# Layer 2 of one group by seven block products, with the steps around it moved

## The chip, the cores and the metric

The kernel runs on one core of a Trainium2 chip. The core has five engines with a queue each, all issuing in order: PE (TensorE, matmul), DVE (VectorE), ACT (ScalarE), POOL (GpSimd) and SP (SyncE, which here only issues DMAs). The metric is device time in microseconds (us) from start to end of one execution; the time of the kernel is the median of its runs. A profile is of one more execution.

## The reference, cut to what matters

```python
B, H, S, D = 8, 8, 576, 64                       # q, k, v: (B, H, S, D), float32
scores = q @ k.T / sqrt(D)                       # kept where 0 <= row - col < 64
attn   = softmax(scores)                         # the rest is masked out
x      = (attn @ v) with heads side by side      # (B, S, 512)
xn     = (x - mean(x)) / sqrt(var(x) + 1e-6) * g_ln
out    = x + relu(xn @ w_ch1) @ w_ch2            # w_ch1: 512 x 2048, w_ch2: 2048 x 512
```

## The kernel before

**Tiling.** Rows are handled in blocks of 128. The first 512 rows of batch b make group b (four blocks, called kb 0 to 3), and the last 64 rows of all eight batches make group 8. Weights are kept in SBUF as f16, with g_ln multiplied into `w1g`; `w2s` holds W2.

**Attention of one block** goes through these steps, each a function that records instructions:
- `cast_qk` (L139), `cast_v` (L172) and `shift_v` (L187) turn loaded f32 tiles into f16 on POOL. `vA` holds V, and `vB` holds V shifted by 64 rows; from batch 2 on `part_vB` (L190) fills `vB` from `vA` with DMAs on SP.
- `t_main` (L252) transposes Q or K on PE and moves the result from PSUM to SBUF, on ACT for Q and on DVE for K where nothing else is said. From batch 3 on Q goes by DMA transpose on SP.
- `s_pe`, `s_exp`, `s_mask` (L307 to L360): scores on PE, exponential on ACT, mask on DVE.
- `b_pe` (L368): probabilities times V on PE. `b_rows` (L390): division by the row sum, then mean and variance, on DVE.
- `z_step` (L416), `z_act` (L441) and `zt_step` (L446): the rows are normalised into z, and z is transposed into `zT`, four pieces of 128 x 128. Groups 0 and 1 only subtract the mean (on DVE, or on ACT for two blocks) and multiply by 1/std after layer 2, since relu lets a positive row factor pass; `root` (L463) computes that factor on POOL. From group 2 on three small POOL steps give 1/std and -mean/std, and z is fully normalised, on ACT in group 2 and on POOL from group 3 on. From group 2 on (`XZ`) `zT` is written by a DMA transpose, apart from block 3 of groups 3 and 5.

**The two layers of one group** come from `mlp_units` (L470) as a list of units for PE:
- Layer 1: `l1` (L477) computes 128 hidden columns for all 512 rows in 4 matmuls of 128 x 512. `l1_half` (L616) computes 256 hidden columns for 256 rows in 8 matmuls of 128 x 256, so that it can start when two blocks of z are there. Both end with a relu on ACT into `hrT`. The argument `split` says for how many of the 16 column groups the halves are used.
- Layer 2, plain: `l2` (L487), 16 matmuls of 128 x 512 for one block of rows, then `add_out` (L498) on DVE and a store. `l2_three` (L629) does three blocks of group 0 side by side.
- Layer 2, by blocks: `stage` (L577) and `product` (L534) do the 512 x 2048 by 2048 x 512 product as a 2 x 2 product of blocks with seven block products in place of eight. `s_sums` (L519) makes the sums of blocks of `hrT` (sS1 to sS4), `w2_sums` (L808) those of W2 (wT2, wT3, wT4, and one in place in `w2s`). Each product is 16 matmuls of 128 x 256, in two units. The order is 4, 1, 2, 6, 5, 7, 3. Products add up in three PSUM banks A, B and C, and `post` and `post_both` (L561 to L573) add a bank to the rows in `x_norm` on DVE before the bank is used again. Stores of row blocks 2 and 3 follow product 7, those of 0 and 1 product 3.

In the kernel before, group 0 uses `l2_three` and `l2`, group 1 `l2`, and groups 2 to 7 the block products. Group 8 has a plan of its own.

**Order.** There is no scheduler: the order on every queue is the order of the calls. The main loop (L934 to L1153) has one period g for each group. Period g runs the units of group g, and after unit i it runs what `at(i, ...)` put into slot i: mostly the attention of batch g + 1 and loads, casts and transposes for batch g + 2. An instruction at the head of a queue that waits holds back all behind it. `queue_up` (L901) puts a long series of loads and POOL casts into slot 0 of period 0.

**PSUM.** There are eight banks. Layer 1 and 2 take turns with two (`mm`), scores have two (`sc`), one pair belongs to `xps`, and two single banks, t0 and t1, serve transposes, one piece of layer 2 of group 0, and bank C. `t_tile` (L72) deals out t0 and t1 in turn, or only t0 where `tbank["shared"]` is set.

Of the kernel before, what the change touches and what calls it, by code (L numbers as in the profile page):

```python
# [18 lines left out]
def kernel(  # L19
# [21 lines left out]
    XZ = 2  # L41
# [87 lines left out]
    def t_two(b, x, half):  # L129
        src = qk16.pop((b, x, half))  # L130
        c0 = 64 * x + 256 * half
        for a in range(2):
            tp = t_tile([128, 4, 128], f"tp_{b}_{x}_{half}_{a}")
            for i in range(4):
                nc.tensor.transpose(out=tp[:, i, :], in_=src[:, 4 * a + i], identity=ident16)
            evac(a, qkT[b][x][:, 2 * a:2 * a + 2, c0:c0 + 256].rearrange("c h (p j) -> c h p j", j=2),
                 tp[:, :].rearrange("c (h j) p -> c h p j", j=2))

# [251 lines left out]
    def b_rows(g, kb):  # L390
# [22 lines left out]
        if g < 2 and (g, kb) not in ((0, 2), (1, 0)):  # L413
            z_step(g, kb)

    def z_step(g, kb):  # L416
# [4 lines left out]
        if g < 2:  # L421
            if (g, kb) not in ((0, 2), (1, 0)):
                nc.vector.tensor_scalar(out=z, in0=xv, scalar1=mu, scalar2=None, op0=ALU.subtract)
            else:
                nmu = p_blk.tile([128, 3], FP32, tag="rsz", name=f"nmu_{g}_{kb}")[:, 0:1]
                nc.vector.tensor_scalar(out=nmu, in0=mu, scalar1=-1.0, scalar2=None, op0=ALU.mult)
                nc.scalar.activation(out=z, in_=xv, func=AF.Identity, bias=nmu, scale=1.0)
            return
# [5 lines left out]
        if g == 2:  # L434
            rsnm[kb] = (rs, nm)
            return
# [4 lines left out]
    def z_act(g, kb):  # L441
        rs, nm = rsnm[kb]
        nc.scalar.activation(out=zsd[(g, kb)], in_=x_norm[(g, kb // 2)][:, kb % 2, :], func=AF.Identity,
                             bias=nm, scale=rs)

    def zt_step(g, kb, eng="act"):  # L446
# [4 lines left out]
        if XZ <= g and not (kb == 3 and g in (3, 5)):  # L451
            nc.sync.dma_start_transpose(out=zT[g][:, :, 128 * kb:128 * kb + 128], in_=z)
            return
# [16 lines left out]
    def mlp_units(g, split=0, three=False, seven=True):  # L470
# [27 lines left out]
        def add_out(kb):  # L498
            xv = x_norm[(g, kb // 2)][:, kb % 2, :]
            if g < 2:  # L500
                nc.vector.scalar_tensor_tensor(
                    out=xv, in0=ch[kb], scalar=rstd[g][:, kb:kb + 1], in1=xv, op0=ALU.mult, op1=ALU.add,
                )
            else:
                nc.vector.tensor_tensor(out=xv, in0=ch[kb], in1=xv, op=ALU.add)
# [395 lines left out]
    def queue_up():  # L901
# [16 lines left out]
        cast_qk(1, 1)  # L918
        cast_v(1, 2, 3)
        shift_v(64, 2)  # L920
        shift_v(0, 2)
        cast_v(1, 3, 4)
        shift_v(64, 3)
        load_qk(2, 0)
        load_qk(2, 1)
        load_v(2, 0, 4)
# [7 lines left out]
    for g in range(NGRP):  # L934
# [4 lines left out]
        units, s_sums = mlp_units(g, (8, 16)[g] if g < 2 else 0, g == 0, g > 1)  # L939
# [14 lines left out]
        if g == 0:  # L954
# [12 lines left out]
            for c in range(2):  # L967
                at(20, vB_cur, 1, c, 0)
                at(20, vB_prev, 1, c, 0)
            at(22, b_pe, 1, 0)  # L970
            at(22, b_rows, 1, 0)
            at(22, z_step, 1, 0)
            at(23, b_pe, 1, 1, "sc")
            at(23, b_rows, 1, 1)
            at(25, zt_step, 1, 0)
            at(25, t_main, 1, 0, 1, 0)
            at(26, lambda: tbank.update(n=0))
            at(26, t_main, 1, 1, 1, 0)
            at(27, zt_step, 1, 1, "dve")
# [3 lines left out]
            at(27, s_exp, 1, 3, 0, 1)  # L983
            at(28, s_mask, 1, 2)
            at(29, s_mask, 1, 3)
        if g == 1:
# [6 lines left out]
            for c in (0, 2):  # L993
                at(0, cast_v, 2, c, c + 2)
                at(5, part_vB, 2, c)
            at(0, t_main, 2, 0, 0)
            at(1, b_pe, 1, 2, "t")
            at(1, b_pe, 1, 3, "sc")
            at(1, b_rows, 1, 2)
            at(1, b_rows, 1, 3)  # L1000
            at(2, root, 1)
            at(2, t_main, 2, 1, 0)
            at(3, t_main, 2, 0, 1)
            at(4, zt_step, 1, 2)
            at(5, t_main, 2, 1, 1)
            at(6, zt_step, 1, 3)
            at(7, w2_sums, 3, 0, 4)
            at(8, w2_sums, 3, 4, 8)
            at(25, w2_sums, 2, 0, 4)
            at(28, w2_sums, 2, 4, 8)  # L1010
            at(9, s_pe, 2, 0)
            at(9, s_pe, 2, 1, False, "xps")
            at(9, s_exp, 2, 0, 0, 1)
            at(10, s_mask, 2, 0)
            at(11, s_exp, 2, 1, 0)
            at(12, s_exp, 2, 1, 1)
            at(13, s_mask, 2, 1)
            for j in range(4):
                i = (14, 17, 20, 22)[j]
                if j < 3:  # L1020
                    at(i, b_pe, 2, j)
                if j < 2:
                    at(i, s_mm, 2, j + 2)
                    at(i + 1, s_mask, 2, j + 2)
                if j == 2:
                    at(i, b_pe, 2, 3, "sc")
                at(i, b_rows, 2, j)
                at(i, z_step, 2, j)
                at((18, 21, 24, 26)[j], z_act, 2, j)
                at((18, 21, 24, 26)[j], zt_step, 2, j)  # L1030
# [11 lines left out]
            first_scores(3, 30)  # L1042
            for i, (x, half) in zip((12, 24, 18, 28), ((0, 0), (1, 0), (0, 1), (1, 1))):
                at(i, t_main, 3, x, half, 0)
# [3 lines left out]
        if g == 2:  # L1048
            for m, i in enumerate((1, 4)):
                at(4 + 2 * m, w2_sums, i, 0, 4)  # L1050
                at(5 + 2 * m, w2_sums, i, 4, 8)
        if g > 1 and b < B:
# [40 lines left out]
            at(12, b_rows, b, 2)  # L1093
            at(12, z_step, b, 2)
            at(19, b_rows, b, 3)
            at(19, z_step, b, 3)
# [24 lines left out]
        if g > 1:  # L1121
# [24 lines left out]
        for i, u in enumerate(units):  # L1146
            if i == (20 if g > 1 else 17 if g == 0 else -1):
# [34 lines left out]
```

## Time and profile before

| | |
|---|---|
| median of 3 runs (lowest, highest) | 302.48 us (302.23, 303.44) |
| profiled execution: time / span from first to last instruction | 302.3 us / 300.3 us |
| busy over the span: PE / DVE / POOL / ACT | 292.2 / 208.4 / 158.4 / 153.9 us |
| mean granted TensorE clock | 0.995 |
| layer 1 of group 1 starts | 53.57 us |
| layer 1 of group 2 starts | 89.45 us |
| DMA: mean rate over the span | 194 GB/s |

The span of period 1, which the change is about, is thus some 36 us. "Busy" is the sum of an engine's instructions; matmuls are pipelined and their ends are modelled, so PE's rates are better taken from rows of many matmuls in the chain of waits, by dividing a row's length by its count. In the timelines a row is start, length, engine, line, operation, output and inputs, count, and in brackets the idle time ahead of it with what ended that.

### The profile page before, as it was taken

The page shows a single profiled execution, that of the slowest core. Times are in us where ns is not written, and L with a number is a line of the kernel's source. Part 1 is how long each engine was busy: PE and PEld are TensorE (multiplying, and loading weights), DVE is VectorE, ACT ScalarE, POOL GpSimd, SP SyncE. Part 2 cuts the span into 40 slices and gives each one's busy share as a digit, 9 for nine tenths or more (in the row PEclk, how much of TensorE's full clock was granted, in tenths as well). Part 3 has the DMA queues.
Part 4 walks back from the last instruction along what each step waited for, and adds up shares of the span by engine and source line. Part 5 has one row for each costly group of instructions (what it writes and reads, how often), then busy time and mean ns, then how long its engine had stood idle before and what let it go on. Part 6 is the DMA issues. An engine that isn't in the chain of part 4 may idle for free.

```text
span 300.3 us, 7568 instructions
## 1 busy us (share of the span) xinstructions
PE 292.2 (97%) x3067; PEld 195.6 (65%) x3067; DVE 208.4 (69%) x409; ACT 153.9 (51%) x259; POOL 158.4 (53%) x234
## 2 busy tenths in 40 slices
PE   8989999999999999999999999999999999999992
PEld 3557545887544588557854786469646854788881
DVE  1781338865937985488858865698667775879972
ACT  2666646676458525873276438841674056216400
POOL 4787877634633876278518860797048307115200
PEclk9999999999999999999999999999999999999997
DMA  7999999989979998999289999992639396013014
GB/s 191 260 382 335 384 286 289 269 266 306 134 194 297 206 187 128 290 248 177 53 265 289 195 160 270 297 163 48 212 72 157 70 232 146 10 38 121 0 38 105
DMA packets 114020, 58.34 MB, mean 194 GB/s; under 512 B 83649, under 2 KB 104705, under 8 KB 113986
## 3 DMA queue, kind: packets, MB, share of 16 engines
q1 hardware_dynamic: 113696, 57.47, 80.0%
q8 instruction: 24, 0.39, 0.6%
q10 hardware_dynamic: 290, 0.40, 0.5%
q14 instruction: 10, 0.08, 0.1%
HBM read 38.80 MB, written 9.44 MB: 161 GB/s over the span
## 4 chain that ended last, share of the span: by engine, by line
PE 95%; ACT 1%; DVE 1%; issue 0%
PE hps L479 31%; PE pA L556 12%; PE pB L556 8%; PE pC L556 8%; PE hph L621 7%; PE ch L491 6%; PE xps L387 4%; PE sc L340 4%; PE ch L638 4%; PE tp L267 3%; PE lA L677 2%; PE warm L848 2%; PE lC L677 1%; PE ztp L456 1%; PE lB L677 1%; ACT pt L350 1%
## 5 line engine op out<-in xcount | busy, mean ns | idle before, releaser
L479 PE MATMUL hps<-zT,w1g 128*128 128x512 f16 x416 | 94.7, 379 | 0.0
L483 ACT ACTIVATE hrT<-hps 128x512 f16<-128x512 f32 x104 | 62.3, 599 | 41.2 <-PE hps L479 37.8
L479 PEld LDWEIGHTS <-w1g 128*128 128x128 f16 x416 | 39.2, 98 | 45.5 <-issue 2.2
L350 ACT ACTIVATE pt<-sc 128x512 f16<-128x512 f32 x72 | 39.3, 600 | 21.4 <-PE sc L340 20.7
L556 PEld LDWEIGHTS <-sS 128*128 128x128 f16 x448 | 43.3, 98 | 5.0
L431 POOL TENSOR_SCALAR rsz<-mvg 128x1 f32<-128x1 f32 x28 | 9.7, 347 | 67.7 <-DVE mvg L412 65.7
L360 DVE TENSOR_TENSOR pt<-pt,mask 128x1024 f16<-128x1024 f16 x32 | 24.7, 776 | 22.3 <-ACT pt L350 22.3
L145 POOL CAST qk<-qk 128x1024 f16<-128x1024 f32 x30 | 33.0, 1114 | 10.3 <-PE hph L621 4.5
L556 PEld LDWEIGHTS <-hrT 128*128 128x128 f16 x336 | 32.1, 98 | 6.4 <-ACT hrT L483 1.0
L248 ACT COPY qkT<-tp 128x1024 f16<-128x1024 f16 (+1 forms) x18 | 17.4, 964 | 24.7 <-PE tp L267 22.4
L556 PE MATMUL pC<-w2s,sS 128*128 128x256 f16 x224 | 26.9, 273 | 0.0
L556 PE MATMUL pA<-wT,sS 128*128 128x256 f16 x224 | 26.9, 273 | 0.0
L407 DVE TENSOR_TENSOR xn<-xps,rcp 128x256 f32<-128x256 f32 (+1 forms) x50 | 25.8, 539 | 1.2 <-DMA out_dram<-xn 0.5
L409 DVE BATCH_NORM_STATS2 stats<-xn 128x6 f32<-128x512 f32 x36 | 25.0, 695 | 1.2
L530 DVE TENSOR_TENSOR sS<-hrT 128x512 f16<-128x512 f16 (+1 forms) x40 | 24.1, 604 | 1.9 <-ACT hrT L483 1.8
L621 PE MATMUL hph<-zT,w1g 128*128 128x256 f16 x192 | 23.4, 273 | 0.1
L437 POOL TENSOR_SCALAR z<-xn,rsz 128x512 f16<-128x512 f32 x24 | 20.7, 862 | 2.5
L403 DVE RECIPROCAL rcp<-xps 128x4 f32<-128x4 f32 (+1 forms) x50 | 7.9, 181 | 18.4 <-PE xps L387 18.4
L432 POOL TENSOR_TENSOR rsz<-rsz,mhalf 128x1 f32<-128x1 f32 x28 | 18.7, 670 | 2.3
L621 PEld LDWEIGHTS <-w1g 128*128 128x128 f16 x192 | 18.1, 98 | 2.9 <-issue 0.2
L491 PE MATMUL ch<-w2s,hrT 128*128 128x512 f16 x80 | 18.8, 380 | 0.0
L387 PEld LDWEIGHTS <-pt 128*64 128x64 f16 x576 | 11.6, 110 | 10.3 <-issue 6.0
(119 smaller groups left out, 427.9 us busy)
## 6 DMA issues: line engine op xcount, KB each, us to landing
out_dram<-xn SPq DMA_DIRECT2D x33, 256.0 KB, 3.2
qk<-in_q_dram SPq DMA_DIRECT2D x16, 512.0 KB, 6.2
qk<-in_k_dram SPq DMA_DIRECT2D x16, 512.0 KB, 7.2
v<-in_v_dram SPq DMA_DIRECT2D x28, 256.0 KB, 6.3
w2s<-in_moe_w_ch_dram SPq DMA_DIRECT2D x9, 512.0 KB, 8.6
w1s<-in_moe_w_ch_dram SPq DMA_DIRECT2D x4, 512.0 KB, 7.2
tk<-in_k_dram SPq DMA_DIRECT2D x8, 256.0 KB, 4.4
tv<-in_v_dram SPq DMA_DIRECT2D x8, 256.0 KB, 4.8
```

Source lines behind the costliest of these rows:

```text
L145: nc.gpsimd.tensor_copy(out=dst[:, :].rearrange("p (a j) e d -> p a e j d", j=j), in_=t[:, :].rearrange("p (a e j d) -> p a e j d", e=2, j ...
L350: nc.scalar.activation(out=o, in_=i, func=AF.Exp, bias=0.0, scale=scale)
L360: nc.vector.tensor_tensor(out=ptv, in0=ptv, in1=mb, op=ALU.mult)
L387: nc.tensor.matmul(out=tiles[h // n][64 * r:64 * r + 64, h % n, :D + 1], lhsT=pt[:, par, hp, r, :], rhs=rhs, start=True, stop=True)
L407: nc.vector.tensor_tensor(out=xn[:, n * i:n * i + n], in0=xps[:, :, 0:D], in1=rcp_b, op=ALU.mult)
L409: nc.vector.bn_stats(out=stats, in_=xv)
L479: nc.tensor.matmul(out=hps, lhsT=w1g[:, kc, 128 * hc:128 * (hc + 1)], rhs=zT[g][:, kc, :], start=(kc == 0), stop=(kc == NKC - 1),)
L483: nc.scalar.activation(out=hrT[:, hc, :], in_=hps, func=AF.Relu, bias=0.0, scale=1.0)
L491: nc.tensor.matmul(out=ch[kb], lhsT=hrT[:, hc, 128 * kb:128 * (kb + 1)], rhs=w2s[:, hc, :], start=(hc == 0), stop=(hc == NHC - 1),)
L530: nc.vector.tensor_tensor(out=o, in0=x, in1=y, op=op)
L556: nc.tensor.matmul(out=o, lhsT=a[:, c, 128 * p:128 * p + 128], rhs=wv[:, c, :], start=(first and (p == 0 or split_c) and c == 0), stop=(c ...
L621: nc.tensor.matmul(out=hps[:, e], lhsT=w1g[:, kc, 128 * hc:128 * (hc + 1)], rhs=zT[g][:, kc, 256 * half:256 * half + 256], start=(kc == 0) ...
```

## The change

- Groups 1 and 2 join the others in being fully normalised before layer 1. In group 1, z of blocks 0 and 2 is made on ACT (`z_act`), that of 1 and 3 on DVE by a new `z_dve`; the three small POOL steps run for group 1 as well, and `root(1)` and the late factor 1/std go.
- Layer 2 of group 1 runs by the seven block products. The sums of W2 that this needs move from periods 1 and 2: half of wT3, wT2 and wT4 into slot 20 of period 0, the other half and the in-place one into slots 7 and 8 of period 1. The sums of `hrT` for group 1 are put into slots 10 to 23, those of group 2 in larger pieces into slots 12 to 18.
- Layer 1 of group 2 runs by halves (`split` 16), and z of its block 3 is transposed on PE in slot 1 of period 2 in place of a DMA transpose.
- In period 0, part of `queue_up` moves into slots 22 and 23, and the cast of batch 1's Q, half 1, goes to ACT (`cast_act`). Transposes of batch 1's Q and K, half 1, come before those of z.
- In period 1, casts and transposes of batch 2 come later, its scores one slot earlier; block 3's `b_rows` and block 2's and 3's z come later. In period 2, `b_rows` and z of blocks 2 and 3 of batch 3 come earlier (slots 8 and 10 in place of 12 and 19).

```diff
+    def cast_act(b, x, half):
...
+        for a in range(2):
+            evac(0, o[:, 2 * a:2 * a + 2], i[:, 2 * a:2 * a + 2])
...
+    def z_dve(g, kb):
+        nc.vector.tensor_scalar(out=zsd[(g, kb)], in0=x_norm[(g, kb // 2)][:, kb % 2, :],
+                                scalar1=mvg[g][:, kb, 0:1], scalar2=rsnm[(g, kb)][0],
+                                op0=ALU.subtract, op1=ALU.mult)
...
-        if XZ <= g and not (kb == 3 and g in (3, 5)):
+        if XZ <= g and not (kb == 3 and g in (2, 3, 5)):
...
-        units, s_sums = mlp_units(g, (8, 16)[g] if g < 2 else 0, g == 0, g > 1)
+        units, s_sums = mlp_units(g, (8, 16, 16)[g] if g < 3 else 0, g == 0, g > 0)
...
+            for i in (3, 2, 4):
+                at(20, w2_sums, i, 0, 4)
...
+            at(22, cast_act, 1, 0, 1)
+            at(22, z_act, 1, 0)
+            at(22, cast_qk, 1, 1, (1,))
+            at(22, load_qk, 2, 1)
+            at(22, load_v, 2, 0, 4)
...
+            at(23, z_step, 1, 1)
...
-            at(25, zt_step, 1, 0)
             at(25, t_main, 1, 0, 1, 0)
+            at(25, z_dve, 1, 1)
             at(26, lambda: tbank.update(n=0))
             at(26, t_main, 1, 1, 1, 0)
-            at(27, zt_step, 1, 1, "dve")
+            at(26, zt_step, 1, 0)
...
+            at(28, zt_step, 1, 1, "dve")
...
-            at(2, root, 1)
-            at(2, t_main, 2, 1, 0)
-            at(3, t_main, 2, 0, 1)
-            at(4, zt_step, 1, 2)
+            at(1, z_step, 1, 3)
+            at(1, t_main, 2, 0, 0)
+            at(3, t_main, 2, 1, 0)
+            at(3, z_dve, 1, 3)
+            at(4, t_main, 2, 0, 1)
+            at(4, z_act, 1, 2)
+            for c in (0, 2):
+                at(4, cast_v, 2, c, c + 2)
+                at(5, part_vB, 2, c)
+            at(5, zt_step, 1, 2)
...
-            at(25, w2_sums, 2, 0, 4)
-            at(28, w2_sums, 2, 4, 8)
...
+            for n, i in enumerate((3, 2, 4)):
+                at(7, w2_sums, i, 4, 8)
+            at(8, w2_sums, 1, 0, 8)
...
+            for c, i in ((0, 10), (2, 12), (4, 14), (6, 16)):
+                at(i, s_sums, c, c + 2, 1, 2)
+            at(19, s_sums, 0, 4, 3)
+            at(21, s_sums, 4, 8, 3)
+            at(23, s_sums, 0, 8, 4)
             for j in range(4):
-                i = (14, 17, 20, 22)[j]
...
+                i = (13, 16, 20, 20)[j]
+                at(i, b_pe, 2, j, "sc" if j == 3 else "xps")
...
+                i = (13, 16, 20, 25)[j]
                 at(i, b_rows, 2, j)
                 at(i, z_step, 2, j)
-                at((18, 21, 24, 26)[j], z_act, 2, j)
-                at((18, 21, 24, 26)[j], zt_step, 2, j)
+                at((17, 20, 25, 29)[j], z_act, 2, j)
+                if j < 3:
+                    at((17, 20, 25)[j], zt_step, 2, j)
...
             at(27, part_vB, 3, 0, 4)
-            first_scores(3, 30)
+            first_scores(3, 28)
...
+            at(1, zt_step, 2, 3)
...
+            for j, i in ((2, 8 if g == 2 else 12), (3, 10 if g == 2 else 19)):
+                at(i, b_rows, b, j)
+                at(i, z_step, b, j)
...
+        if g == 2:
+            for c, i in ((0, 12), (4, 16)):
+                at(i, s_sums, c, c + 4, 1, 2)
+                at(i + 2, s_sums, c, c + 4, 3, 4)
```

## The prediction

> **What bounds the kernel now.** I read the chain of waits first, then the costliest groups, then the timelines of PE, ACT, DVE and SP between 45 and 125 us, where the change lies.
>
> ```profile
> PE 95%; ACT 1%; DVE 1%; issue 0%
> ...
> 78.44 3.56 PE ch L491 x16
> ...
> 82.44 3.45 PE ch L491 x16
> ...
> 98.71 7.01 PE hps L479 x32
> ...
> 109.77 1.75 PE pB L556 x16
> ```
>
> These are shares of the chain that ended last, and pieces of it (start, length, instructions). PE is the path, and its rates can be read off: 3.45/16 = 0.216 us for a 512-wide matmul of layer 2, 7.01/32 = 0.219 for one of layer 1, 1.75/16 = 0.109 for a 256-wide one. A microsecond of PE work saved is worth a microsecond, unless PE then waits for somebody.
>
> ```profile
> 24.00 4.37 PE hph L621 x40
> ...
> 62.80 0.60 ACT hrT L626
> 63.40 0.49 ACT zT L459
> 63.93 1.91 PE hph L621 x16
> ```
>
> Same view. A layer 1 matmul by halves costs 4.37/40 = 0.109, half of a whole one. At 63.93 PE starts on rows 256-511 of group 1 (mark 1), having waited for ACT to bring the last transposed block.
>
> ```profile
> 59.56 1.01 ACT L248 COPY qkT<-tp 128x1024 f16<-128x1024 f16 x1
> ...
> 76.16 0.81 ACT L443 ACTIVATE z<-xn,rsz 128x512 f16<-128x512 f32 x1
> ```
>
> ACT's timeline: what an evacuation of Q or K and a normalisation on ACT cost.
>
> ```profile
> 87.11 0.53 SPq L517 DMA_DIRECT2D out_dram<-xn  x1
> 87.74 0.49 SPq L192 DMA_DIRECT2D vB<-vA  x1
> 88.28 0.59 SPq L194 DMA_DIRECT2D vB<-vA  x1
> 90.43 0.34 SPq L517 DMA_DIRECT2D out_dram<-xn  x1
> 90.82 0.43 SPq L92 DMA_DIRECT2D qk<-in_q_dram  x1
> ```
>
> SP's queue at the end of period 1: it issues in order, 0.6 us each. The copy into vB that batch 3's first b_pe reads goes out at 87.74, and by the table of DMA issues such a copy lands 3.2 us after its issue:
>
> ```profile
> vB<-vA SPq DMA_DIRECT2D x5, 260.0 KB, 3.2
> 92.27 0.22 PE L387 MATMUL xps<-vB,pt 128*64 128x65 f16 x1
> ```
>
> So it is there at 90.9, 1.3 us before PE reads it at 92.27 (mark 2).
>
> **PE's own work.** Layer 2 of group 1 loses 64 matmuls of 512 (64 x 0.216 = 13.80) and gets 112 of 256 (112 x 0.109 = 12.25): -1.55. Group 2's layer 1 by halves: 64 x 0.219 = 14.0 against 128 x 0.109 = 14.0, so 0. The fourth zT block of group 2 goes from a DMA transpose to four PE transposes: +0.22 (four took 62.60 to 62.83). All of it is on the path: **-1.33**.
>
> **Up to mark 1.** Before, PE has from 48.01 to 63.93 instructions worth 15.2 us (16 matmuls of 512, 64 of 256, 16 + 48 transposes at 0.055, two scores and two b_pe at 0.3 each), so it waits 0.7 there. In the new order:
> - Batch 1's last Q and K transposes come before the first z transpose, whose PSUM bank (t1) still holds ch of block 2. DVE frees it in add_out, behind the statistics of block 1, which end at 49.6 before; two add_outs took 1.39, so one is done at about 50.3. Dropping nmu saves 0.1 of it. PE asks at 49.76 (48.01 + 0.44 + 0.87 + 0.44): 0.55 to 0.6 of wait. The three small POOL steps for 1/std, at 1.2 to 1.5 in all (80.18 to 81.4 and 94.80 to 96.6 in POOL's timeline), end by 48.5 and delay K's cast by at most 0.2; both hide behind the bank.
> - The second layer 1 unit wants the bank of ch block 3. Its add_out now stands behind the z copy and a mask on DVE: about 55.05 against 54.85 wanted, 0.2. A mask takes 0.68 alone (54.93) but 1.47 at 52.88, beside a cast on POOL; if it meets one, this wait is 0.9.
> - z of block 2 moves from DVE to ACT, behind the evacuation of Q's half 1. From the end of that transpose ACT needs 0.15 for the relu in front, 0.9, and 0.81, together 1.9; PE has one unit (0.87) to do meanwhile: 1.0 of wait. What is late next are the zT copies, 0.1 more before mark 1.
>
> Waits of 1.9 in place of 0.7: **mark 1 comes 1.2 later**, with 1.0 to 1.9 as bounds. W2's sums cost nothing: three stand between DVE's mask end at 40.94 and its next row at 45.03, 2.0 us in a hole of 4.1; the other five (the last two as one) follow at about 64.5, where DVE before did only two and then had 2.58 idle (to 67.48), and the mask behind them is read by PE only at 71. Without those holes each is 0.65. The moved batch 2 loads keep their place in SP's queue.
>
> **From mark 1 to mark 2.** Rows that DVE now does between 71 and 89: four b_rows at 1.8, two masks at 0.66, sums of 3.6 in all (a 128x1024 sum is 0.66, 512 wide 0.4, the new 2048 wide one estimated at 1.25), four posts at 0.6, and before them two more of each kind: 15 us of DVE for some 15 of PE, in an order written out. Before, it was busy 3.58 of 4 us at most there. So DVE becomes level with PE and each post comes just in time or late: the second use of bank B at 77.45 meets its post's end at about 77.9. I take 0.6 for such waits (0 to 1.5).
>
> A rule speaks against this stage: the Trainium skill, "SBUF — State Buffer", section "Who interferes with whom", says that a two-input VectorE operation on SBUF and a GpSimd operation reading SBUF shut each other out for a whole instruction. By the rows the meeting costs 0.8 (1.47 against 0.68); by the rule up to one cast, 1.04. Four casts fall here; if two of them met a sum or mask ahead of a post that is just in time, the total would grow by 1.6 by the rows and by 2.1 by the rule.
>
> With -1.55 for the products and +0.6, product 3 ends at about 89.1, 0.5 ahead of before (89.61). Then:
> - z of block 3 on ACT waits for 1/std (its statistics end near 88), and stands between batch 3's two score exponentials, two of 0.5 each. Relu of the next unit follows at 91.0-91.5, where the third unit wants its bank at 90.6-90.9: about 0.7.
> - The copy into vB. It stays at slot 27, but product 7's unit 27 now puts the stores of blocks 2 and 3 on SP in front of it, and these wait for post_both. Product 7 ends near 86.8 on PE; DVE comes to post_both 1.5 later, behind b_rows of block 3 (1.8); 1.23 for it (L565 at 117.46); two issues 1.25; landing 3.2. 86.8 + 1.5 + 1.23 + 1.25 + 3.2 = 94.0 for mark 2, against 91.9 by PE alone. It swallows the 0.7. Behind this wait on PE stand batch 3's scores and ACT's exponentials of them; behind the stores on SP, the loads for batch 4.
>
> **Mark 2 comes 1.7 later** than before (92.27 to 94.0; 0 with DVE on time and the shortest landing of 2.7, 3.0 with the longest of 4.7 and DVE 2 late).
>
> **After mark 2.** Loads for batch 4 go out behind four stores instead of one: about 93 against 90.82, with 0.75 MB more ahead of them. DMA was 0.81 to 1.18 busy in each 4 us of 92-116, so the lag stays. The second DMA transpose of batch 4's Q was issued near 111.8 and lands by 116.9 (longest landing about 5), where PE wants it at 117.42: slack 0.5, then PE's own 1.7 later. +0.3 (0 to 1.5). Group 2's earlier b_rows and fewer, larger sums lie on DVE beside PE: 0.
>
> Sum against the profiled execution, 302.3 (span 300.3 plus 2.0 around it, 0.2 under the median of 302.48): +1.7 + 0.3 = **304.3**. The -1.33 is inside the 1.7.
>
> **Rivals.**
> 1. *vB in time: not slower.* If DVE keeps level and post_both ends by 87.3, the copy is issued by 88.6 and lands by 91.9, when PE asks. Then only the waits up to mark 1 stay: 1.2 - 1.33 plus about 0.3 of bank waits = +0.2: 302.5. For it: DVE was 69% busy over the span. Against it: post_both stands behind b_rows, 1.8, in the same queue. It decides from post_both's end at 87.3.
> 2. *The PE saving arrives whole, and the old 0.7 of waits goes too:* 302.3 - 1.33 - 0.7 = 300.3. Against it: the z on ACT behind the Q copy is an order, not a matter of luck.
> 3. *The DMA stream runs late:* four stores in front of the loads, Q's transpose at 119-121, +1.5 on top of 304.3: 305.8. For it: DMA share near 1 and a slack of 0.5. Against it: later periods of before also put their stores there and PE did not stop; one z transpose less.
>
> **How the numbers follow.** The forecast 304.3 has a chance of 0.50 (own range 303.2 to 305.2), rival 1 0.28, rival 2 0.06, rival 3 0.16. A measurement tells this kernel from no change at about 0.5%, 1.5 us (300.97 to 303.99). Of the forecast 0.08 falls inside that, of rival 1 0.01 on the faster side: faster 0.07, same 0.35, slower 0.58. The range goes from under rival 1 to over rival 3: 301.8 to 306.0.
>
> **What would show it.** In the changed profile: products of 1.75 per 16 and no L491 in period 1; a PE wait at the z transpose of block 0 for DVE, and one of 1.0 at block 2 for ACT; SP's vB issue after two stores, later than 89; b_pe of batch 3 waiting for a DMA. Wrong is the forecast if vB is issued before 88.6, if ACT does z of block 2 ahead of Q's copy, or if posts run level with PE.

## The result, and the profile after

The changed kernel is slower: 306.99 us in the median of 4 runs (306.68 to 307.57) against 302.37 for the kernel before on the same chip, a ratio of 1.0149 [1.0127, 1.0171], so the 1.5% is clear of the noise. The profiled execution took 306.75 (span 305.0). The forecast was 304.3 with a range up to 306.0: the direction held, the size did not. The steps that failed are the end of the program, the idle time before mark 1, a slip in the sum for mark 2, and the price of what moved in period 2.

The same pieces of work, found in both profiled executions:

| reached at (us) | before | after | later by | forecast |
|---|---|---|---|---|
| mark 1 (rows 256-511 of group 1 on PE) | 63.93 | 65.70 | 1.77 | 1.2 |
| mark 2 (first b_pe of batch 3) | 92.27 | 95.09 | 2.82 | 1.7 |
| first score of batch 4 | 117.35 | 120.46 | 3.11 | 2.0 |
| last row of DVE | 294.63 | 297.98 | 3.35 | 2.0 |
| end of the span | 300.29 | 305.02 | 4.73 | 2.0 |

Mark 1 of the changed kernel is taken as one unit, 1.1 us, behind the first unit after the last z transposes. First the chain of waits: the shares from the page, then pieces of the chain (start, length, what).

```profile
PE 78%; DVE 9%; SPq 4%; DMA 4%; ACT 2%; issue 1%; POOL 1%
...
61.05 1.01 ACT qkT L257
62.05 0.72 ACT z L452
...
78.75 0.57 DVE xn L580
79.33 1.20 DVE pt L369 x2
...
88.81 0.70 DVE stats L418
...
89.72 1.12 DVE xn L576
90.86 0.35 SPq L528
...
91.27 0.54 SPq L528
...
91.92 3.14 DMA vB<-vA
...
95.09 0.45 PE xps L396 x16
```

PE was 95% of this chain before. Now the chain leaves PE at Q's evacuation on ACT, and runs on DVE nearly without a break from 71.3 to 90.8, then through two stores on SP and the copy into vB, until PE reads that copy at 95.09: mark 2 is set by DVE and SP.

PE's waits over the whole span of the changed kernel (line that waited, releaser; total, times, longest):

```profile
PE ztp L470 <- ACT z L452: 1.0, 1, 1.0
PE hph L632 <- ACT hrT L637: 0.9, 1, 0.9
...
PE xps L396 <- DMA vB<-vA: 0.6, 1, 0.6
PE pB L567 <- DVE xn L580: 0.5, 1, 0.5
...
PE hph L632 <- DVE xn L514: 0.4, 1, 0.4
```

None of these five is in the kernel before. Each costs some 0.15 more than listed, since the end of the matmul ahead of a wait is modelled. This timeline of PE, after, shows it (start, length):

```profile
74.29 1.10 PE L567 MATMUL pB<-wT,hrT 128*128 128x256 f16 x8
...
76.93 1.91 PE L567 MATMUL pA<-w2s,hrT 128*128 128x256 f16 x16
79.38 1.03 PE L567 MATMUL pB<-w2s,hrT 128*128 128x256 f16 x8 [0.54 <-DVE xn L580]
...
90.43 1.91 PE L632 MATMUL hph<-zT,w1g 128*128 128x256 f16 x16
```

In an unbroken stream 16 such matmuls start 1.75 us before the next instruction, so the second half of the second product was due at 76.93 + 1.75 = 78.68 and came at 79.38: 0.70 late, where 0.54 is listed. The same rows give the length of group 1's layer 2 with the attention steps inside it: 74.29 to 90.43, 16.14 us. Before it was 72.49 to 89.45, 16.96.

That stretch, engine by engine (start:end length, then busy time and instructions of PE, PEld, DVE, ACT, POOL; clock; DMA share; GB/s), of the kernel before and of the changed one:

```profile
72.49:89.45 16.96, 16.96 (x179) 8.66 (x176) 10.43 (x23) 7.96 (x13) 8.68 (x16) 1.00 0.94 171
```

```profile
74.29:90.43 16.14, 15.60 (x226) 13.33 (x224) 15.73 (x32) 6.89 (x10) 9.36 (x15) 1.00 0.73 113
```

PE's busy time falls by 1.36 (1.5 with the modelled end), DVE's rises by 5.3, to 15.73 of 16.14. PE's saving was bought with a second engine that has no time left.

### The profile page after: what moved, and what is told of

Its sections match the earlier page's. It is cut to its first block, busy times and chain, and to the rows that moved or that the text cites. A ratio compares the mean times of both kernels' runs of the same rounds, so it can differ in the third digit from the quotient of the medians.

```text
span 305.0 us, 7812 instructions
## 1 busy us (share of the span) xinstructions
PE 291.0 (95%) x3183; PEld 206.2 (68%) x3183; DVE 218.3 (72%) x416; ACT 156.6 (51%) x263; POOL 162.4 (53%) x243
## 4 chain that ended last, share of the span: by engine, by line
PE 78%; DVE 9%; SPq 4%; DMA 4%; ACT 2%; issue 1%; POOL 1%
PE hps L493 26%; PE pA L567 12%; PE pB L567 8%; PE pC L567 8%; PE hph L632 8%; PE xps L396 3%; PE sc L349 3%; PE ch L649 3%; DMA w1s<-in_moe_w_ch_dram 3%; PE lA L688 2%; PE tp L276 2%; DVE sS L541 2%; SPq L176 2%; DVE xn L416 1%; DVE stats L418 1%; SPq L87 1%
## 5 line engine op out<-in xcount | busy, mean ns | idle before, releaser
L493 PE MATMUL hps<-zT,w1g 128*128 128x512 f16 x352 | 80.2, 379 | 0.1
L497 ACT ACTIVATE hrT<-hps 128x512 f16<-128x512 f32 x88 | 52.8, 599 | 37.0 <-PE hps L493 33.9
L493 PEld LDWEIGHTS <-w1g 128*128 128x128 f16 x352 | 33.1, 98 | 38.2 <-issue 2.0
L567 PEld LDWEIGHTS <-sS 128*128 128x128 f16 x512 | 49.4, 98 | 5.7
L567 PEld LDWEIGHTS <-hrT 128*128 128x128 f16 x384 | 36.6, 98 | 7.7 <-issue 1.0
L632 PE MATMUL hph<-zT,w1g 128*128 128x256 f16 x320 | 38.1, 273 | 1.5 <-ACT hrT L637 0.9
L632 PEld LDWEIGHTS <-w1g 128*128 128x128 f16 x320 | 30.5, 98 | 6.2 <-issue 1.8
L567 PE MATMUL pC<-w2s,sS 128*128 128x256 f16 x256 | 31.1, 273 | 0.0
L541 DVE TENSOR_TENSOR sS<-hrT 128x512 f16<-128x512 f16 (+1 forms) x44 | 28.2, 640 | 1.9 <-ACT hrT L497 1.8
L637 ACT ACTIVATE hrT<-hph 128x512 f16<-128x512 f32 x40 | 23.8, 599 | 11.0 <-PE hph L632 10.6
L182 POOL CAST vA<-v 128x1024 f16<-128x1024 f32 (+1 forms) x18 | 17.1, 966 | 4.3 <-DMA v<-in_v_dram 4.0
```

The costliest lines, as they stand in the source:

```text
L493: nc.tensor.matmul(out=hps, lhsT=w1g[:, kc, 128 * hc:128 * (hc + 1)], rhs=zT[g][:, kc, :], start=(kc == 0), stop=(kc == NKC - 1),)
L497: nc.scalar.activation(out=hrT[:, hc, :], in_=hps, func=AF.Relu, bias=0.0, scale=1.0)
L541: nc.vector.tensor_tensor(out=o, in0=x, in1=y, op=op)
L567: nc.tensor.matmul(out=o, lhsT=a[:, c, 128 * p:128 * p + 128], rhs=wv[:, c, :], start=(first and (p == 0 or split_c) and c == 0), stop=(c ...
L632: nc.tensor.matmul(out=hps[:, e], lhsT=w1g[:, kc, 128 * hc:128 * (hc + 1)], rhs=zT[g][:, kc, 256 * half:256 * half + 256], start=(kc == 0) ...
L637: nc.scalar.activation(out=hrT[:, 2 * i:2 * i + 2, 256 * half:256 * half + 256], in_=hps, func=AF.Relu, bias=0.0, scale=1.0)
```

## The experiments

In all of them the kernel before ran beside the others, on the same chip: medians of 302.38 to 302.69. Times are medians; "last row" is the start of DVE's last row, "end" what the span has behind it.

| kernel | mark 2 | batch 4's score | last row | end | median |
|---|---|---|---|---|---|
| before | 92.27 | 117.35 | 294.63 | 5.7 | 302.4 |
| after | 95.09 | 120.46 | 297.98 | 7.0 | 306.99 |
| after, again (d1_again) | 94.98 | 120.26 | 297.72 | 7.1 | 307.18 |
| vB ahead (a1_vb) | 94.41 | 119.60 | 296.96 | 6.7 | 305.35 |
| z on DVE (a2_z2) | 94.84 | 120.10 | 298.71 | 6.0 | 306.04 |
| three cures (a3_all) | 92.98 | 118.17 | 295.71 | 5.6 | 303.50 |
| three cures, both moved, plain layer 2 (a5_plain) | 93.01 | 118.19 | 295.46 | 5.7 | 302.90 |
| three cures, mask moved (a8_mask) | 92.77 | 117.96 | 296.11 | 5.6 | 303.48 |
| three cures, rows moved (a9_rows) | 92.52 | 119.28 | 297.62 | 5.7 | 305.06 |
| three cures, both moved (a4_fix) | 92.72 | 119.87 | 297.88 | 5.7 | 305.42 |
| and loads first (a6_loads) | 92.68 | 125.17 | 302.52 | 5.7 | 310.32 |
| and a sum on POOL (a7_pool) | 92.69 | 126.59 | 303.86 | 5.6 | 311.46 |
| before, halves (c3_halves) | 92.11 | 117.54 | 294.81 | 5.7 | 302.89 |
| before, DVE padded (b1_pad) | 93.39 | 118.48 | 295.74 | 5.6 | 302.18 |
| before, ACT padded (b2_actpad) | 92.10 | 117.18 | 294.51 | 6.6 | 303.17 |
| after, ACT padded (d2_afterpad) | 95.18 | 120.37 | 298.45 | 6.1 | 305.78 |

### The waits up to mark 2

The copy into vB one slot earlier, which puts it ahead of the stores on SP:

```diff
-            at(27, part_vB, 3, 0, 4)
+            at(26, part_vB, 3, 0, 4)
```

> The changed kernel with part_vB of batch 3 one slot earlier (26 in place of 27), so that SP issues the copy into vB ahead of the stores of group 1's row blocks 2 and 3. Theory (the wait of 0.63 us of PE at batch 3's first b_pe, after 3.14 us of DMA, is SP's order: stores that wait for post_both stand in front): the copy is issued at 88 to 90 in place of 91.92, PE no longer waits for a DMA there, and PE is 0.6 us earlier from there on: span 304.4, time about 306.4. The wait of 0.87 for ACT just before it stays. Rival (DVE sets the pace there, the DMA is only what came last): less than 0.2 us gained.

z of group 1's block 2 on DVE:

```diff
+            at(3, z_dve, 1, 2)
             at(3, z_dve, 1, 3)
...
-            at(4, z_act, 1, 2)
```

> The changed kernel with z of group 1's block 2 made by DVE (slot 3, ahead of block 3's) in place of ACT behind the evacuation of Q. Theory (the 0.98 us wait of PE at that block's transpose is ACT's order): the wait goes, layer 1 of rows 256-511 starts 0.9 to 1.0 us earlier (64.7 in place of 65.70), and what follows moves with it: span 304.0, time 306.0. Rival (DVE, continuously busy from 71.3 to 90.8, sets the time of the copy into vB whatever PE does before): the 1.0 us is seen at 65 and lost again by 95, time as the changed kernel, 306.9.

Both, and z of group 2's block 3 on POOL (`z_step` makes it there, and its `z_act` is left out):

```diff
-        if g < 3:
+        if g < 3 and (g, kb) != (2, 3):
             rsnm[(g, kb)] = (rs, nm)
             return
...
-                at((17, 20, 25, 29)[j], z_act, 2, j)
+                if j < 3: at((17, 20, 25)[j], z_act, 2, j)
```

> The changed kernel with both edits, and z of group 2's block 3 on POOL in place of ACT between the exponentials of batch 3. Theory (three waits of 0.98, 0.87 and 0.63 us are all queue order, and add up): PE ends 2.3 to 2.5 us earlier than in the changed kernel, span 302.6, time 304.5; still above the kernel before by what the end of the program adds (1.3 us after PE's end) and by about 0.8 of bank and DVE waits. Rival (DVE level with PE in layer 2 of group 1): less than 1.2 us gained, and PE waits for posts instead.

With vB ahead, SP issues the copy at 88.64 in place of 91.92, PE's wait of 0.63 is gone and mark 2 comes 0.68 earlier, as the wait said it would. The median fell by more, 1.64: in the profiled executions the last row comes 1.02 earlier and the end is 0.4 shorter. z on DVE takes away the 0.98 (mark 1 at 64.72), but the wait for the first post of the block products grows from 0.54 to 1.27 and swallows 0.73 of it: layer 1 of group 2 starts only 0.24 earlier (90.19 for 90.43), and mark 2 moves by 0.25. Later this execution waited 0.67 for a DMA transpose of Q and 0.35 for one of z, so that its last row came later than that of the changed kernel. Yet its median fell by 0.95, the figure expected: its end is 1.1 shorter, for ACT's count of instructions and not for z (below), so that the agreement is luck. All three cures together bring mark 2 from 95.09 to 92.98 and the time to 303.50, 1.0033 [1.002, 1.0046] of before. That is 1.0 less than expected, because the end is short here too (5.6), but not below the kernel before.

What is left with all three (PE's waits, the lines that the kernel before does not have):

```profile
PE pB L567 <- DVE xn L580: 1.0, 1, 1.0
...
PE hph L632 <- DVE xn L514: 0.4, 1, 0.4
```

The wait for the first post of the block products has doubled, from 0.54 to 1.03: PE comes earlier, DVE does not.

### Are the block products worth it there?

Layer 2 of group 1 plain again; rows stay fully normalised. The in-place W2 difference goes back to period 2. The version this was made of is not that with three cures alone, as the expectation says with its 303.5: it also has the two edits of order shown further down, of the mask and of `b_rows` (a4_fix, 305.42).

```diff
-        units, s_sums = mlp_units(g, (8, 16, 16)[g] if g < 3 else 0, g == 0, g > 0)
+        units, s_sums = mlp_units(g, (8, 16, 16)[g] if g < 3 else 0, g == 0, g > 1)
...
-            at(8, w2_sums, 1, 0, 8)
...
-            for c, i in ((0, 10), (2, 12), (4, 14), (6, 16)):
-                at(i, s_sums, c, c + 2, 1, 2)
-            at(19, s_sums, 0, 4, 3)
-            at(21, s_sums, 4, 8, 3)
-            at(23, s_sums, 0, 8, 4)
```

> The same version with group 1's layer 2 as 64 matmuls of 512 again, on the fully normalised rows, without that group's sums, and with the in-place W2 difference back in period 2. Theory (the block products save 64 x 0.216 - 112 x 0.109 = 1.55 on PE): PE from layer 2's first matmul to group 2's first layer 1 matmul, without attention steps, 1.55 longer; about 1.3 to 1.6 slower than the version it is made of (303.5). Rival (the saving is eaten by posts and sums on DVE): within 0.5 of it, or faster.

It takes 302.90, where the theory wanted it 1.3 to 1.6 slower, so the rival holds. The version with the products and all the same edits, on the same chip, is 2.5 slower, mostly for loads that come late (below). Against the best versions with products, 303.50 and 303.48, the ratios to the kernel before are 1.0018 [1.0007, 1.0028] here and 1.0033 [1.002, 1.0046] and 1.0027 [1.0008, 1.0046] there: not told apart. The layer 2 stretch with three cures, with three cures and the mask moved, and with plain layer 2 (columns as above):

```profile
73.38:90.04 16.66, 15.63 (x226) 13.34 (x224) 16.25 (x32) 7.00 (x10) 9.43 (x15) 1.00 0.78 138
```

```profile
72.94:89.83 16.89, 15.64 (x227) 13.33 (x224) 16.45 (x34) 7.00 (x10) 9.43 (x15) 1.00 0.91 145
```

```profile
73.04:90.00 16.96, 16.96 (x178) 8.64 (x176) 9.80 (x21) 7.88 (x12) 9.38 (x17) 1.00 1.08 200
```

With the products PE's work is 1.33 shorter by the list, yet the stretch is shorter by 0.30 only, and DVE is busy 16.25 of 16.66. The plain version came to this stretch 0.34 earlier, since the mask edit takes a wait of 0.4 before mark 1 away; the version that has this edit and the products (second row) needs 16.89 for the stretch, 0.07 less than plain layer 2.

Two edits of order, to take both waits for DVE away from the version with three cures. One puts a mask behind the add_out that PE waits for, the other puts `b_rows` of batch 2's block 1 behind the first post:

```diff
-            at(28, s_mask, 1, 2)
+            at(29, s_mask, 1, 2)
```

```diff
-                i = (13, 16, 20, 20)[j]
+                i = (13, 16, 21, 21)[j]
                 at(i, b_pe, 2, j, "sc" if j == 3 else "xps")
...
-                i = (13, 16, 20, 25)[j]
+                i = (13, 17, 21, 25)[j]
                 at(i, b_rows, 2, j)
...
-            for i, (x, half) in zip((12, 21, 18, 24), ((0, 0), (1, 0), (0, 1), (1, 1))):
+            for i, (x, half) in zip((12, 20, 18, 24), ((0, 0), (1, 0), (0, 1), (1, 1))):
```

Both together, then each alone:

> The version with all three cures (303.5) and two more of order alone: the mask of batch 1's step 2 is put behind the add_out that frees the second layer 1 unit's bank, and b_rows of batch 2's block 1 behind the first post of the products, with b_pe of blocks 2 and 3 one unit later. Theory (PE's own work is 1.33 shorter, and what is left over 302.5 is two waits for DVE, 0.41 and 1.03 as listed, some 0.15 more each because ends of matmuls are modelled): 1.4 to 1.7 go, up to 0.4 of new wait at b_pe comes: 302.1 (301.7 to 302.5), not slower than before. Rival (DVE has no room in this stage, and its lateness only moves to the next post): 303.0 to 303.6.

> The version with three cures (303.5) and of the two further edits of order the first alone: the mask of batch 1's step 2 behind the add_out that frees the second layer 1 unit's bank. Theory (that wait is 0.41 as listed and 0.15 more, and the loss of the fully cured version came from the other edit): mark 1 0.5 earlier, 302.9 to 303.1. Rival (this edit set off the late loads): a PE wait of 1 or more for POOL's cast near 113, 304 or more.

> The same version with the second of the two edits alone: b_rows of batch 2's block 1 behind the first post of the products, b_pe of blocks 2 and 3 one unit later. Theory (this moves DVE's lateness to the later posts, and the stores and with them batch 4's loads go out later): waits for posts 0.5 to 0.8 in all in place of 1.03, a PE wait near 113 for POOL's cast, 304.5 to 305.5. Rival (the other edit did it): 302.5 to 303.3 and no wait near 113.

Here my theory fell: 305.42 in place of 302.1, 303.48 and 305.06 for the single edits. The mask alone does bring mark 1 0.44 earlier, and all of it is lost: the post wait grows from 1.03 to 1.25, and one of 0.59 for a DMA transpose of z comes behind batch 4's scores. In the execution with both, mark 1 is not earlier (64.75): PE waited 0.41 for a cast of W2 at 45.26, ahead of the change's waits. The rows alone cure the first post, but 0.51 of wait comes back at a later one and the loads of batch 4 turn late. PE's waits in the version with both:

```profile
PE tp L276 <- POOL qk L154: 2.3, 2, 1.8
...
PE pA L567 <- DVE xn L580: 0.7, 2, 0.5
```

The 1.8 is at 112.94, where PE wants a transpose of batch 4's K and POOL has not cast it yet. The version with the rows alone waits 1.39 at the same place, that with the mask alone does not wait there, so the rows' edit is the cause. SP issued these loads only 0.4 later than in the version with three cures (93.47 against 93.07), and POOL's cast came 1.9 later (113.64 against 111.77): POOL first waited 1.46 for half 1 of Q to land, and then its three z steps stood in front. Why a load issued 0.4 later lands that much later stays open.

The loads put ahead of the four stores on SP, and then one of DVE's sums on POOL as well:

```diff
-            at(40, load_qk, 4, 0)
-            at(40, load_qk, 4, 1)
+            at(26, load_qk, 4, 0)
+            at(26, load_qk, 4, 1)
```

```diff
-                nc.vector.tensor_tensor(out=o, in0=x, in1=y, op=op)
+                (nc.gpsimd if g == 1 and n == 3 and c0 == 4 else nc.vector).tensor_tensor(out=o, in0=x, in1=y, op=op)
```

> The fully cured version (305.4) with batch 4's Q and K loads on SP in front of the four output stores of group 1. Theory (there the loads were issued behind the stores at 93.5, half 1 of Q landed 1.5 after POOL wanted it, and PE waited 1.8 for K's cast and 0.4 for a transposed block of z): these two waits go; from the first b_pe of batch 3 to batch 4's first score 25.1 to 25.4 in place of 27.15; median 302.9 to 303.5. Rival (the DMA stream is late for its bytes, not for its order): 27 again, 305.

> The same with one of DVE's sums of group 1 (128x1024) on POOL. Theory (DVE is the bound of the block products: in the fully cured version PE waited 0.51 and 0.15 for two posts, while DVE had no idle time from 75 to 92): DVE gains some 0.7 to 1.1, the 0.51 before the seventh product goes, 0.4 to 0.7 less than the version with the loads alone, 302.2 to 302.9. Rival (POOL's sum holds up DVE or the casts behind it): no gain, or up to 1 slower.

Both came out far slower, for a cause that neither theory had. DVE's timeline with the loads first (in brackets: idle before, and releaser):

```profile
93.17 0.21 DVE L412 RECIPROCAL rcp<-xps 128x8 f32<-128x8 f32 x1 [0.72 <-PE xps L396]
101.69 0.69 DVE L416 TENSOR_TENSOR xn<-xps,rcp 128x512 f32<-128x512 f32 x1 [8.31 <-DMA out_dram<-xn]
```

`b_rows` of batch 3 writes into the buffer that the stores read, so with 2 MB of loads in front of them DVE stood for 8.3 us and PE for 4.2. The waits for POOL and for the DMA transpose did go, but the run can't say what the order of the loads is worth in all. With the sum on POOL, PE's wait of 0.51 for a post in the block products went (one of 0.15 stayed), and a new one of 0.9 for POOL's z came. The layer 2 stretch ends before DVE's stop, and there the sum's move can be read; with the loads first, then with the sum on POOL as well:

```profile
73.24:89.74 16.50, 15.83 (x226) 13.49 (x224) 16.06 (x34) 7.00 (x10) 9.56 (x15) 1.00 0.81 142
```

```profile
72.86:88.62 15.76, 15.61 (x226) 13.51 (x224) 15.32 (x33) 7.00 (x10) 11.71 (x15) 1.00 0.88 142
```

One sum less on DVE shortens the stretch by 0.74, to 0.15 above PE's own work and 1.20 under the 16.96 of the kernel before. So DVE is what holds the products up; whether that gain would last to the end was not tried without the loads in front.

### Layer 1 of group 2 by halves

On the kernel before, this part alone (with that group's sums and `b_rows` where the change has them):

```diff
-        units, s_sums = mlp_units(g, (8, 16)[g] if g < 2 else 0, g == 0, g > 1)
+        units, s_sums = mlp_units(g, (8, 16, 16)[g] if g < 3 else 0, g == 0, g > 1)
```

> The kernel before with one part of the change alone: group 2's layer 1 by halves (128 matmuls of 256 for 64 of 512), with that group's sums and b_rows where the change has them. Theory (halves cost PE nothing, 128 x 0.109 = 64 x 0.219): 302.5 (302.2 to 302.8), from the first b_pe of batch 3 to batch 4's first score 25.1 as before. Rival (each half costs, and is the 0.29 by which that stretch grew in the changed kernel): stretch 25.4, 302.8 to 303.0. Rival (more PE instructions make the program's end longer): 303.0 to 303.6 with the span's end over 6.5 behind DVE's last row.

The numbers are those of the first rival: the stretch from mark 2 to batch 4's score is 25.43 against 25.08, and the median 302.89 against 302.38, 1.0017 [1.0007, 1.0028]. But the halves are only a part of it. PE before, then PE and POOL with the halves:

```profile
111.35 1.04 PE L556 MATMUL pA<-wT,sS 128*128 128x256 f16 x8
112.22 0.61 PE L267 MATMUL tp<-ident,qk 128*128 128x128 f16 x8
```

```profile
111.29 1.04 PE L556 MATMUL pA<-wT,sS 128*128 128x256 f16 x8
112.40 0.62 PE L267 MATMUL tp<-ident,qk 128*128 128x128 f16 x8
```

```profile
111.30 1.04 POOL L145 CAST qk<-qk 128x1024 f16<-128x1024 f32 x1
```

Before, the transposes of batch 4's K start 0.87 after the unit ahead of them, here 1.11, just behind POOL's cast (111.30 + 1.04 = 112.34). This wait of 0.24 is too short for the list, as ends are modelled. In front of the cast POOL now has z of batch 3's blocks 2 and 3, whose `b_rows` this edit moves from slots 12 and 19 to 8 and 10; the cast is in slot 11. From the scores of batch 3 to layer 2 PE takes 12.45, 0.11 more than before. In the changed kernel the stretch is 25.37, of which the same wait is 0.17 (transposes 1.04 after the unit ahead); in the cured ones it is 25.18 to 25.19, without the wait. So by the timelines the halves cost 0.1, not 0 and not 0.29, and the earlier `b_rows` the rest.

### The end of the span

The changed kernel needs 1.38 us more from DVE's last row to the end, for the same stores. A first guess was DVE's program, which has ten instructions more: ten one-element memsets at the start of the kernel before.

> The kernel before with ten one-element memsets on DVE at the start, where DVE is idle, so that DVE's queue has as many instructions as in the changed kernel (480 for 470). In the changed kernel 1.35 us of the 4.7 us lie after PE's last matmul, with two instruction fetches there that the kernel before does not have. Theory (a queue whose program crosses a block of instructions near its end fetches that block in the last microseconds, and DVE's is the one): DVE shows it: an instruction fetch after the last store, span 1.0 to 1.4 us longer, time 303.4 to 303.8, while PE ends as before (294.6). Rival (it is POOL's or ACT's queue, or the end of PE's longer program, or chance of that execution): time within 0.3 us of the kernel before.

Nothing: 302.18 (its profiled execution was its slowest, 303.64, with two waits for a cast of W2 ahead of the change's place, and its end was short). Then the changed kernel again, for a second profile:

> The changed kernel unchanged, for a second profiled execution. Its first one ended 7.0 us after DVE's last row began (297.98 to 305.0), the kernel before 5.7 (294.63 to 300.3): SP's last wait for the last store 4.5 against 3.5, its last wait for PE 0.8 against 0.4. Theory (that end is a chance of one execution, since the store is the same): DVE's last row near 298.0 again, the span ends 5.5 to 6.2 behind it, and the median is 306.0 to 306.5. Rival (the longer end belongs to the program): 6.6 to 7.2 again, median 306.7 to 307.3.

It has the long end again (7.1), so it is no chance. The DMA queues while the last stores run (packets, MB, share; then issues with the time to landing) in the kernel before and in the changed one:

```profile
q10 hardware_dynamic: 288, 0.39, 32.8%
...
out_dram<-xn SPq DMA_DIRECT2D x1, 128.0 KB, 3.9
out_dram<-xn ACTq DMA_DIRECT2D x1, 128.0 KB, 4.1
```

```profile
q10 hardware_dynamic: 286, 0.39, 33.8%
q14 instruction: 1, 0.01, 0.5%
...
out_dram<-xn SPq DMA_DIRECT2D x1, 128.0 KB, 4.0
out_dram<-xn ACTq DMA_DIRECT2D x1, 128.0 KB, 5.1
```

One fetch of instructions, 8 KB and 0.3 us, falls among the packets of the last store, which lands 1.0 later; why by more than the 0.3 of the fetch stays open. It is there in the three profiles with the 5.1 us landing, all of programs with 324 instructions on ACT, and in none with 322 or 323 (the cured versions) or 317 (before); the traces record two fewer of each. So copies of one element were put on ACT in the middle of group 4, where it waits for PE: seven on the kernel before (324), twelve on the changed one (336).

```diff
+        if g == 4:
+            for i in range(7):
+                at(2 + i, lambda: nc.scalar.copy(out=pad, in_=mhalf[0:1, 0:1]))
```

> The kernel before with seven one-element copies on ACT in the middle of group 4, where ACT waits for PE: 324 instructions on ACT, as many as the changed kernel has (the kernel before 317; the two cured versions whose end was short 323 and 322). In the changed kernel's traces an instruction fetch of 8 KB lies among the packets of the very last store, whose completion comes 1.0 us later. Theory (ACT's instruction count puts that fetch there): the span's end 6.5 to 7.1 behind DVE's last row in place of 5.7, SP's last wait for the store 4.5, the last row where it was (294.6); median 303.2 to 303.9. Rival (the count of ACT has nothing to do with it): end 5.5 to 6.0, 302.2 to 302.7.

> The changed kernel with twelve such copies on ACT in group 4 (336 instructions on ACT), which moves ACT's instruction fetches away from the last store if they are the cause. Theory: SP's last wait for the store 3.5 again, the span's end 5.6 to 6.3 behind DVE's last row (297.7 to 298.0), median 305.8 to 306.3. Rival (the longer end has another cause): 4.5 and 6.6 to 7.2 again, 306.7 to 307.3.

Both theories hold, with the medians a hair below their ranges. SP's last waits with seven copies on the kernel before, then with twelve on the changed one:

```profile
SPq L1181 <- DMA out_dram<-xn: 4.4, 1, 4.4
SPq L1181 <- PEq L1181: 0.6, 2, 0.4
```

```profile
SPq L1205 <- DMA out_dram<-xn: 3.5, 1, 3.5
SPq L1205 <- PEq L1205: 1.0, 2, 0.8
```

The kernel before gets the long wait and 0.7 us (303.17), with its last row where it was. The changed kernel loses the long wait and 1.2 to 1.4 us (305.78), though nothing else in it is better. What stays is the 0.8 for PE's queue (0.4 before) at the end. No run was made for that 0.4; it is 0.4 again in all versions with the vB copy one slot earlier, and 0.7 to 0.8 in all profiles of the changed kernel without that edit. Why is open.

## Why the prediction was wrong

Right were the direction, the places and kinds of nearly all waits, and PE's own work: predicted -1.55 for layer 2, measured -1.36 by the list and -1.5 with the modelled end. Its profiled time missed by 306.75 - 304.3 = 2.45, and the terms are these:

1. **The end of the program, predicted 0, measured 1.38.** This is the step that failed outright: the forecast had nothing behind PE's last instruction. The cause of 1.0 of it is shown: seven instructions more on ACT move a fetch into the last store. The Trainium skill, "Runtime: NRT & Kernel Launch", section "Instruction fetch mechanics", says that a sequencer fetches its next block over a DMA queue of its own while it runs, and that crossing a block is mostly hidden. Ahead of the end the traces agree: the changed kernel's profile has 36 fetches (25 on queue q8, 11 on q14), and no listed wait of PE is put down to one. At the end nothing is left to hide it. That page's blocks are of 16 KiB; those on q14 are of 8 KB here.
2. **Mark 1, predicted 1.2, measured 1.77.** The new waits are as predicted in sum, 1.9 against 1.53 as listed or some 2.0 with the modelled ends: 0.98 for z on ACT (predicted 1.0), 0.42 for the second layer 1 unit (0.2, or 0.9 beside a cast), 0.13 for the first z transpose (0.55 to 0.6). What failed is "in place of 0.7": the idle time that I took out of the old stretch was an instruction sum priced too low (15.2), and only some 0.2 went away: the list has no PE wait there in the kernel before, and the changed one needs 17.69 for the same work with its 2.0 of waits, which leaves 15.7. That is 0.5 of the 0.57.
3. **Mark 1 to mark 2, predicted 0.5, measured 1.05.** The mechanism was right and shown by the first cure: copy behind stores, stores behind post_both, post_both behind `b_rows`. From the seventh product's end on PE (88.0) to DVE's end of post_both it took 2.8 (predicted 2.73), from there to the landing 4.2 (4.5). What failed was the start, 88.0 in place of 86.8, and first by a slip in the sum: with the forecast's own terms (1.2 to mark 1, -1.55, +0.6) product 3 ends at 89.61 + 0.25 = 89.86, and 89.1 is written. This 0.75 is missing in product 7's 86.8 and so in mark 2; without the slip the forecast would have been some 305.1. The miss at mark 1 added 0.57, and the first post 0.1 (0.70 late where 0.6 stood for all posts); these three make 1.4, a little more than the 1.2 by which the start was late.
4. **After mark 2, predicted 0.3, measured 0.53,** and 0.29 by batch 4's score. The cause named, a late transpose of Q, did not occur in the changed kernel. Two terms put at 0 failed instead: the halves, 0.10, and the earlier `b_rows`, 0.17 of wait for POOL's cast of K. The 0.24 after batch 4's score was not traced. Late loads are real one step on: order edits in the cured version set them off.
5. The time around the span was 1.73, not 2.0: -0.27. That this made up for a part of the rest was luck.

Rival 1 (vB in time, only the waits up to mark 1 left, 302.5) was made into a kernel: with vB ahead alone it is 305.35, because z on the rows of batch 2, the halves, the posts and the end stay. The forecast said that DVE "becomes level with PE"; the consequence drawn, 0.6 for late posts, was too mild. The runs show more: of what was given back to PE in front of that stage (z, the mask), half or more returned as a longer wait at the first post: 0.54 in the changed kernel, 1.27 with z on DVE, 1.03 with three cures, 1.25 with the mask moved as well. No version of the change beat the kernel before.

One rule was weighed in the prediction: a two-input VectorE operation on SBUF and a GpSimd operation reading SBUF shutting each other out (the Trainium skill, "SBUF — State Buffer", section "Who interferes with whom"). The 2048-wide sum met two casts in the changed kernel. DVE's timeline there, and that of the version with both edits of order, where POOL had no cast beside it, only its steps of one column:

```profile
85.58 1.72 DVE L541 TENSOR_TENSOR sS<-hrT,sS 128x2048 f16<-128x2048 f16 x1
```

```profile
85.48 1.22 DVE L541 TENSOR_TENSOR sS<-hrT,sS 128x2048 f16<-128x2048 f16 x1
```

The meeting cost DVE 0.50, and POOL's two casts took 3.02 in place of 2.02. By the rows it delays both sides; the rule's full exclusion of one cast, 1.04, was not reached on DVE.

## What to carry to other kernels

Work saved on the engine that bounds the kernel is worth its price only while the engine that pays for it has slack in the same stretch: read the busy time of both there (here DVE went from 10.4 of 17.0 to 15.7 of 16.1), not over the span. When PE waits for an engine without slack, moving instructions in its queue moves the wait; test it with a version that also undoes the saving. Look at the end of the program apart from the rest: a handful of instructions on an engine that does not bound the kernel can move an instruction fetch into the last store (here seven on ACT; ten on DVE moved none), and the 0.3% that this costs will look like an effect of the edit, as in the run with z on DVE.

## What the runs showed of the hardware

- One 8 KB instruction fetch among the packets of a 128 KB store put off its landing from 4.1 to 5.0 or 5.1 us, in three programs; seven more instructions on ACT, at a place where it waits, switched it on in the kernel before, and twelve more switched it off in the changed one.
- PE's wait of 4.2 us in the version with the loads first halved its clock for a while. Windows of that run (columns as above, the clock is the third number from the end):

```profile
98.00:99.00 1.00, 0.25 (x3) 0.11 (x1) 0.00 (x0) 0.74 (x2) 0.00 (x0) 1.00 1.04 365
100.00:101.00 1.00, 0.00 (x0) 0.00 (x0) 0.00 (x0) 0.00 (x0) 0.00 (x0) 0.90 1.05 406
101.00:102.00 1.00, 0.00 (x0) 0.00 (x0) 0.31 (x1) 0.00 (x0) 0.00 (x0) 0.50 1.06 376
107.00:108.00 1.00, 1.00 (x8) 0.78 (x7) 0.93 (x3) 0.60 (x1) 1.00 (x2) 0.69 0.56 129
108.00:109.00 1.00, 1.00 (x11) 0.90 (x10) 1.00 (x5) 0.60 (x1) 1.00 (x2) 1.00 0.11 23
```

PE's last matmul ended at 98.25; a mean of 0.90 in the second window puts the fall to 0.50 at 100.8, 2.6 us later, and 0.69 in the fourth puts the return to 1.00 at 107.6. From 103 on these 4.6 us at half clock are, by estimate, 2.3 us of full clock, on top of the wait. In the version with the sum on POOL PE waited 5.1 us, and the clock fell 4.5 us after PE's last matmul. The waits of up to 1 us in the changed kernel's layer 2 and around it left the clock at 1.00. The Trainium skill, "TensorE: Matmul & The Clock Gate", section "What's actually happening", has the clock fall to half after at least one idle window of about 3.4 us. The fall 4.5 us after the last matmul agrees; that after 2.6 us does not, so a shorter stop was enough here.
